# New order lists for the last first-gate steps and the second gate of a Nystrom-attention and two-gate kernel

## The chip, the cores and the metric

One core of a Trainium2 chip runs the whole program. The metric is the device time in microseconds (us) of one execution. The engines are TensorE (PE, with its weight loads PEld), VectorE (DVE), ScalarE (ACT), GpSimd (POOL) and SyncE (SP), which here issues nearly all DMA transfers. A measurement of a change gives the median of several executions.

## The reference, cut to what matters

```python
# attention, Nystrom, per batch (4) and head (8), 576 rows of 64
A, Bm, C = softmax(q @ k_lm.T / 8), softmax(q_lm @ k_lm.T / 8), softmax(q_lm @ k.T / 8)
...
x = (A @ Z @ C @ v)                     # Z: six Newton steps on Bm
x = x.transpose(0, 2, 1, 3).reshape(2304, 512)
h = x @ moe_w_in                        # 512 -> 2048, first gate
x = (h * cos(h)) @ moe_w_out            # 2048 -> 512
h = x @ moe2_w_in                       # second gate
x = (max(h, 0) + alpha * min(h, 0)) @ moe2_w_out
```

Inputs are float32; weights arrive in 64-bit form and are converted on the chip.

## The kernel before, in words

Everything is computed as split float32: each operand is a high part (ACT copy to a rounded float32) and a low part (a subtraction), and each product is three matmuls, high x high, high x low, low x high.

**Order by hand-made list.** The program creates all operations first, each with a key such as `b12:9`: the context before the colon, the running number of the operation within it behind. `Plan.go` (L331) then emits them in the order of the string `ORDER` (L20), one queue for each engine following from it. A suffix `/V`, `/A` or `/G` puts an operation with a choice on DVE, ACT or POOL; without one the first choice of the operation is taken. A tile's buffer is given when its first operation is emitted, in turn within its ring (the lists of `place`, from L428 on), so the order also decides which earlier tile an operation must wait for. Each engine and SP's DMA queue work strictly in list order: a waiting instruction holds back all behind it.

**First gate, contexts t0 to t127 (`tick`, L1087).** A tick makes 128 hidden units for 288 tokens: `t:1` six matmuls into an "h" bank (two banks), `t:2` to `t:7` cos and split on ACT, DVE and POOL, `t:8` to `t:11` three matmuls each into four "acc" banks. Contexts `e` store the sums to the scratch tensor y1d, `c` convert the second gate's weights.

**Second gate, contexts b0 to b39.** The 2304 tokens are cut into four chunks of 512 and one of 256, eight steps each: b0 to b7 chunk 0, b8 to b15 chunk 1 (`btick`, L1744, with `strassen`, L1449), b16 to b31 chunks 2 and 3 (`mtick`, L1546, with `narrow`, L1494), b32 to b39 the last (`mtick`). A step makes 256 hidden units by seven Strassen-like products of six 256-column matmuls each (L1465 or L1509), which must keep their sequence. Copies of partial sums (L409 on ACT, L411 on DVE) and additions on DVE (L1488, L1521) lie between them: in `strassen` the products are numbers 1, 2, 4, 5, 7, 9, 10 and 3, 6, 8, 11 are copies, 12 and 13 additions; in `narrow` the products are 1, 2, 5, 7, 9, 10, 12 and 11 an addition. The activation follows on DVE and ACT, then the second product: for b0 to b15 eight groups of three 512-column matmuls (L1778, numbers 18 to 21 and 26 to 29), later seven products (L1660). In the last chunk a step has two products of twelve matmuls (L1564, numbers 1 and 2) and seven of three (19 to 25).

**Loads of the second gate.** The first chunk makes seven forms of the input weights for every two steps (`s_load`, L1262, contexts s64 to s67): load from wi2d (L1271), high part on ACT (L1251), low part and sums (L414, L1285), and a store of each form to wf2d (L1281). Chunks 1 to 3 load these forms back, 512 KB each (`f_load`, L1307, contexts s68 to s76), into a ring "sr" of seven buffers. So a form's load can start when the last product of the step before has read its buffer. `y_load` (contexts y0 to y4) brings the tokens of a chunk and makes their seven combinations. `load_wo2` (o0 to o15) and `t_make` (x0 to x7, loads at L1413) prepare the output weights; they use a ring "f" of four buffers, which the output copies and stores of chunks 0 and 1 (L1790) use too. In b7, for instance, the four output copies are b7:27, 30, 33, 36 and their stores b7:28, 31, 34, 37.

**End.** `y_end` (L1704) adds the last products on DVE (b39:27 to b39:33, L1720) and stores through SP and ACT.

Of the kernel before, what the change touches and what calls it, by code (L numbers as in the profile page):

```python
# [129 lines left out]
c62:3 t105:7 t108:1 t104:10 t103:9 t106:4 t108:2 t106:5 t106:6 c58:4 t104:9 t103:11 t104:11 t105:11 t108:3 t108:4 t107:1  # L130
t107:2 t107:3 t107:4 t103:8 t105:9 t106:7 t106:11 t108:5 c57:1 t107:5 t107:6 t107:7/V t104:8 t110:1 t105:8 c58:5 t108:6
t110:2 e95:3 c63:2 c62:4 t105:10 t109:1 t110:3 t108:7/V s64:22 c57:2 t110:4 t109:2 t110:5 t110:6 c63:3 t109:3 c57:3
s64:26 t106:9 t106:8 t106:10 t107:11 t108:11 t111:1 t107:8 s64:15 t109:4 t109:5 t111:2 t107:9 t108:9 t108:8 t112:1
t109:6 t109:7/V t109:8 t111:3 t111:4 s64:16 t110:7 t107:10 t108:10 c57:4 t111:5 t109:11 t110:11 t114:1 t112:2 t112:3
t112:4 c63:4 s64:27 t111:6 t112:5 t114:2 t112:6 t113:1 t109:10 t110:10 t109:9 t110:9 t111:7 t111:10 y0:2 t113:2 t113:3
t113:4 s64:28 t112:7 t114:3 t114:4 t110:8 t111:11 t111:8 s64:19 s64:20 t113:5 t114:5 t113:6 e111:5 e111:4 t114:6 t116:1
c57:5 y0:1 t111:9 e111:1/V e111:2/V y0:21 y0:22 t116:2 y0:16 t113:7 y0:3 t115:1 t115:2 t112:11 t112:9 t112:10 s64:17
c63:5 e111:6 y0:4 t114:7 t113:11 t112:8 t113:10 t116:3 t116:4 t116:5 t115:3 t115:4 t115:5 y0:5 s64:13 s64:23 t115:6 y0:7
y0:17 t115:7 t113:8 t117:1 t114:10 t114:11 t119:1 t113:9 t114:9 t114:8 t115:9 t115:8 t115:10 t117:2 t117:3 y0:36 y0:31
t116:6 t119:2 t117:4 y0:23 s64:24/V t119:3 t116:7/V t119:4 y0:11 t117:5 t118:1 y0:12 y0:6/V t119:5 t118:2 t117:6 t117:7  # L140
y0:32/V y0:13/V t118:3 t118:4 t118:5 t118:6 t115:11 t116:11 t116:8 t116:9 t120:1 t117:9 t119:6 t121:1 t118:7 t117:11
t118:11 y0:14 t120:2 t121:2 o1:1 y0:24 s64:21 y0:25 y0:26 y0:33 y0:37/V y0:8/V s64:10 e111:3 t119:7/V t120:3 t116:10
y0:38 t120:4 t120:5 t121:3 t120:6 s65:2 s64:29 t121:4 t121:5 t117:8 t117:10 t121:6 t119:11 o9:1 t122:1 t120:7/V y0:18
t118:9 t119:9 t123:1 o1:2 t122:2 y0:9 y0:29 t121:7/V t122:3 t118:10 t119:10 t118:8 t120:10 t119:8 t122:4 t123:2 y0:10/V
t122:5 t123:3 y0:34 y0:15/V t123:4 t123:5 y0:39 t122:6 y0:35/V o9:2 t122:7 y0:30 y0:19 t123:6 t123:7 t120:8 t120:9
t121:10 t121:9 t124:1 t122:9 t125:1 t121:8 t120:11 t123:9 o1:3 t121:11 t124:2 t124:3 t124:4 t124:5 y0:27 t127:1 t122:8
t125:2 t125:3 t125:4 y0:20 s65:3 o9:3 t125:5 y0:40/V y0:28/V t124:6 t127:2 t127:3 t122:10 t123:10 t122:11 t126:1 t123:8
t124:7/V t124:8 t123:11 t127:4 t127:5 t127:6 t126:2 t125:6 o10:1 c62:5 o11:1 s64:25 s65:1 o0:1 t125:7 t127:7/V t126:3
# [6 lines left out]
b0:25 b0:20 b1:15 b1:22 b1:16 s66:1 b2:11 b0:18 b3:4 b3:5 s66:4 s66:2 b1:23 o6:3 b1:17/G b2:12 b3:3/V s66:11 b1:24 b3:6  # L155
s65:29 e127:6 s66:8 b0:19 b3:7 s66:12/V s66:13 o3:1 e127:3 b2:22 b3:8 s66:5 b3:9 s66:6 b1:25/G s66:9/V s66:14/V s66:15
s66:16/V b2:23 b3:10 b3:11/V b2:14 s66:18/V s66:17 s66:22 s66:10 s65:21 o2:1 b0:26 b1:18 s66:26/V o3:2 s66:27 s66:23
s66:24 b2:15 s66:28/V o12:1 s66:7 b0:28 b3:13 b2:24 b2:16 s66:19 s66:20 s67:2 b0:27 b4:1 b0:29 o2:2 b2:25/G b1:19 b1:21
b4:2 b4:3/V b4:4 b4:5 b1:27 b1:20 b1:28 s67:1 b3:12 b2:17/G s66:29 s66:25 b4:7 b4:6 b1:26 s67:3 b4:8/V b4:9 b4:10 b1:29
b5:1 b5:2 b5:4 s67:4 b4:13 o2:3/V b2:19 b5:5 b3:14 b3:15 o3:3/V s67:8 b3:16 b3:17/G o14:1 s66:21 b4:11/V b5:3/V b2:18  # L160
b2:21 b2:20 b2:27 b2:28 b3:20 s67:5 b3:22 b4:12 b4:22 b3:23 b5:6/V s67:11 s67:12/V b3:24 s67:6 b4:23 s67:9/V s67:14/V
b3:25 b4:14 b5:7 s67:15 b5:8 b5:9 s67:18 s67:22 o13:1 o13:2 s67:16/V o13:3/V s67:26/V b2:29 b3:21 b5:10 b6:1 b3:19 b2:26
b3:18 s67:23 b4:24 o12:2 b6:2 b3:29 b4:15 s67:24/V b5:11 b4:16 o12:3/V o14:2 b5:12 b5:13 o14:3 s67:19 s67:27 b6:4 b3:26
b3:27 b6:3/V b6:5 b6:7 b3:28 s67:20/V s67:28/V b6:6/V b6:8 b6:9 b6:10 b7:1 s67:17 y1:1 b4:25 b4:17 b5:14 b5:15 b5:22
o5:1 o5:2 y1:2 b5:16 y1:3 b6:13 b5:17 b4:20 b7:2 b7:4 b7:5 y1:16 b7:3 b6:11/V b4:21 b4:29 b7:6/V b6:12 b5:23 y1:4 y1:11
y1:5 b6:14 b6:15 y1:17/V s67:25 y1:22 y1:21 s67:21 b7:7 b4:28 b7:9 y1:12/V o5:3 y1:23 y1:24 y1:6 b7:8 y1:36 y1:13/V
y1:25/V y1:31 y1:32/V y1:37/V y1:26/V y1:9 y1:27 o15:1 o7:1 b5:24 b5:25 y1:10/V b7:10 b4:18 b4:19 b7:11 b4:26 b5:21 b8:1
b4:27 b5:19 b5:18 b6:16 b6:17/G b8:2 y1:14 y1:18 y1:19 y1:7 y1:29 o7:2 y1:33/V b6:22 y1:20/V b7:12 y1:38/V y1:15/V y1:39
# [10 lines left out]
b12:5 b9:28 b12:7 b12:6 b12:8 b12:9 b10:20 b12:10 b13:1 b13:2 b13:4 s70:1 b12:11 x6:7 b12:13 x5:3/V x6:6/V x6:9 b12:12
b10:18 b9:27 x6:10/V b12:14 x6:8 y2:2 s70:2 x4:1 x4:2 b10:19 b13:5 x5:4/V b13:3 s70:3 b10:28 x5:5 x5:6 b10:21 b10:29  # L180
b13:7 s70:4 b12:15 b12:16 x5:7 b13:6 b13:9 b12:22 b12:17 b13:8/V b12:23 b10:27 b11:20 b13:10 b10:26 b11:21 b11:18 b11:26
b14:1 b12:24 s70:7 x5:8 x5:9 x5:11 x4:3 x4:4 x4:5 x4:6 x5:12 x4:7 x4:9 b11:19 b14:2 b13:11 b13:12 b13:13 s70:6 x3:2
b14:3/V b13:22 b12:25 x4:10/V b13:23 b14:4 b11:27 x5:10 x4:8 b14:5 y2:1 b14:6 s70:5 b14:7 b13:24 b11:28 b14:9 b14:8
# [1665 lines left out]
```

## Time and profile before

| | |
|---|---|
| runs, median of 3 | 795.76 us (794.31 to 796.95) |
| profiled execution, own time | 791.91 us |
| its span, first to last instruction | 790.1 us |
| granted TensorE clock, mean | 0.999 of full |
| instructions | 18146 |
| DMA | 154.81 MB, mean 196 GB/s |

In the views used below, a line is "line of the source, engine, operation, output tile <- input tile, shape, count". All tiles in SBUF are called m; acc, h and x are PSUM banks. The timeline gives start, duration, and in brackets the engine's idle time before with what ended it. The chain of waits is the run of work that ended last, followed back; "SPq" is SP's issue of a DMA. In the table of stretches each engine has its busy time and, in brackets, its instructions.

### The profile page before, as it was taken

How to read it: one execution, taken by the hardware profiler on the slowest of the kernel's cores; microseconds unless marked ns; L12 is line 12 of the kernel's file. 1: busy time of each engine (PE TensorE's matmuls, PEld its weight loads, DVE VectorE, ACT ScalarE, POOL GpSimd, SP SyncE). 2: the span in 40 equal slices, each digit the busy share in tenths (PEclk: the TensorE clock that was granted, in tenths of full speed). 3: DMA queues.
4: the chain of work that ended last, by engine and by line, in shares of the span. 5: the costliest groups of instructions: out<-in, count | busy, mean ns of one | idle time of the engine just before them, and what ended most of it. 6: DMA issues, size and time to landing. Idle time of an engine off the chain costs nothing. (4 is left out here: it accounts for less than half of the span.)

```text
span 790.1 us, 18146 instructions
## 1 busy us (share of the span) xinstructions
PE 775.1 (98%) x6906; PEld 713.9 (90%) x6906; DVE 637.6 (81%) x1382; ACT 440.3 (56%) x998; POOL 247.5 (31%) x264
## 2 busy tenths in 40 slices
...
GB/s 294 258 277 135 124 162 161 201 200 184 280 196 243 308 167 264 231 213 170 156 213 270 280 205 118 257 244 256 50 214 223 215 47 144 189 204 122 131 199 28
DMA packets 114279, 154.81 MB, mean 196 GB/s; under 512 B 55568, under 2 KB 73488, under 8 KB 114192
## 3 DMA queue, kind: packets, MB, share of 16 engines
...
q10 hardware_dynamic: 160, 0.26, 0.1%
HBM read 114.57 MB, written 39.06 MB: 194 GB/s over the span
## 5 line engine op out<-in xcount | busy, mean ns | idle before, releaser
L414 POOL TENSOR_TENSOR m<-m,m 128x288 fp32r<-128x288 f32 (+4 forms) x183 | 181.8, 1007 | 440.3 <-ACT m L1115 136.0
L1128 PE MATMUL acc<-m,m 128*128 128x288 f32 x1536 | 230.7, 297 | 0.0
L1128 PEld LDWEIGHTS acc<-m,m 128*128 128x128 f32 x1536 | 210.7, 188 | 14.6 <-issue 10.8
L414 DVE TENSOR_TENSOR m<-m,m 128x512 fp32r<-128x512 f32 (+5 forms) x261 | 145.6, 579 | 27.4 <-ACT m L1613 12.3
L1103 PE MATMUL h<-m,m 128*128 128x288 f32 x768 | 124.8, 299 | 0.6 <-DVE m L1113 0.4
L1103 PEld LDWEIGHTS h<-m,m 128*128 128x128 f32 x768 | 108.0, 188 | 7.0 <-DVE m L1113 4.0
L1778 PE MATMUL acc<-m,m 128*128 128x512 f32 x384 | 97.6, 392 | 0.0
L1112 ACT ACTIVATE m<-m,quarter 128x288 f32<-128x288 f32 x128 | 67.5, 534 | 39.7 <-DVE m L1110 39.0
L1509 PE MATMUL x<-m,m 128*128 128x256 f32 x588 | 84.8, 284 | 0.8 <-DVE m L414 0.6
L1778 PEld LDWEIGHTS acc<-m,m 128*128 128x128 f32 x384 | 68.2, 188 | 11.6
L1509 PEld LDWEIGHTS x<-m,m 128*128 128x128 f32 x588 | 75.5, 188 | 3.3 <-ACT m L409 1.0
L1113 DVE TENSOR_TENSOR m<-m,h 128x288 f32<-128x288 f32 x128 | 57.3, 450 | 25.6 <-ACT m L1112 19.9
L1613 ACT ACTIVATE m<-m 128x256 fp32r<-128x256 f32 (+2 forms) x96 | 45.8, 508 | 54.5 <-DVE m L1627 20.5
L1110 DVE SCALAR_TENSOR_TENSOR m<-h,m 128x288 f32<-128x288 f32 x128 | 57.3, 451 | 19.9 <-ACT m L1108 19.0
L1660 PE MATMUL acc<-m,m 128*128 128x256 f32 x485 | 70.0, 283 | 0.1
L1108 ACT ACTIVATE m<-h 128x288 int32<-128x288 f32 x128 | 51.7, 404 | 33.1 <-PE h L1103 31.4
L1115 ACT ACTIVATE m<-m 128x288 fp32r<-128x288 f32 x128 | 55.3, 439 | 26.1 <-DVE m L1113 21.7
L1660 PEld LDWEIGHTS acc<-m,m 128*128 128x128 f32 x485 | 63.2, 191 | 0.5 <-ACT m L1613 0.3
L409 ACT ACTIVATE m<-x 128x256 f32<-128x256 f32 (+6 forms) x80 | 31.1, 399 | 45.4 <-PE x L1509 28.5
L579 DVE SCALAR_TENSOR_TENSOR m<-m,m 128x512 int32<-128x512 int32 x64 | 46.8, 737 | 0.3
L577 DVE SCALAR_TENSOR_TENSOR m<-m,m 128x512 int32<-128x512 int32 x64 | 44.3, 697 | 0.4
L1465 PE MATMUL h<-m,m 128*128 128x256 f32 x300 | 42.7, 281 | 1.2 <-ACT m L409 1.2
(182 smaller groups left out, 1125.6 us busy)
## 6 DMA issues: line engine op xcount, KB each, us to landing
m<-wf2d SPq DMA_DIRECT2D x72, 512.0 KB, 5.0
m<-in_moe_w_in_dram SPq DMA_DIRECT2D x32, 512.0 KB, 6.0
m<-in_moe_w_out_dram SPq DMA_DIRECT2D x32, 512.0 KB, 5.9
wf2d<-m SPq DMA_DIRECT2D x28, 512.0 KB, 4.4
...
```

The source lines that it names most:

```text
L414: ENG[e].tensor_tensor(o, a, b, op=ALU.subtract)
L579: op(dve(512), lambda e: nc.vector.scalar_tensor_tensor(cf.t, rv(0), 29, cf.t, op0=ALU.logical_shift_right, op1=ALU.bitwise_or), r=[raw], ...
L1103: nc.tensor.matmul(out=hp.t[:, 0:CW], lhsT=w_[:, js], rhs=x[:, cs], start=(i == 0), stop=(i == 5))
L1108: op(act(CW, True), lambda e: nc.scalar.activation(k_.t, hp.t[:, 0:CW], AF.Copy, scale=INV2PI, bias=0.25), r=[hp], w=[k_], target=T + 0.8)
L1110: op(dve(CW), lambda e: nc.vector.scalar_tensor_tensor(u.t, hp.t[:, 0:CW], INV2PI, k_.t, op0=ALU.mult, op1=ALU.subtract), r=[hp, k_], w=[u])
L1112: op(act(CW), lambda e: nc.scalar.activation(u.t, u.t, AF.Sin, scale=2.0 * math.pi, bias=quarter), rw=[u], aset="sin")
L1113: op(dve(CW), lambda e: nc.vector.tensor_tensor(hc.t, u.t, hp.t[:, 0:CW], op=ALU.mult), r=[hp, u], w=[hc], target=T + 2.6)
L1115: op(act(CW), lambda e: nc.scalar.activation(gh.t, hc.t, AF.Copy), r=[hc], w=[gh, gl])
L1128: nc.tensor.matmul(out=yg[o].t[:, 0:CW], lhsT=w_.t[:, sl], rhs=x.t, start=(j == ja and i == 0), stop=(j == jb and i == 2),)
L1509: nc.tensor.matmul(out=rv(r), lhsT=a_.t[:, p, c2, js], rhs=b_.t[:, q_, c2], start=(first and c2 == 0 and y == 0), stop=(c2 == 1 and y == 2 ...
L1660: nc.tensor.matmul(out=yb.t[:, 256 * (p + yh):256 * (p + yh) + 256], lhsT=a_, rhs=b_, start=(st and p + yh + y == 0), stop=(en and y == 2) ...
L1778: nc.tensor.matmul(out=ya[n][t].t, lhsT=gv(x_), rhs=r_.t, start=(st and k == 0), stop=(en and k == 2))
```

## The change

Only the string `ORDER` changes, from the 2153rd of its 4254 entries on (in the middle of tick 104). Both lists hold the same operations; 171 of them also change engine: 67 from DVE to POOL, 54 from POOL to DVE, 25 from DVE to ACT and 25 from ACT to DVE. On each engine the operations from the first difference on, before and after, and how many of them can be kept in their relative order: PE 651 and 651 product groups, 328; DVE 677 and 664, 316; ACT 466 and 466, 239; POOL 107 and 120, 41; SP 196 and 196, 93. The diff, cut to whole lines around the steps spoken of below:

```diff
@@ -127,124 +127,124 @@
...
-b0:12 b0:14 o11:3/V o10:3 t125:8 b1:1 o4:1 s65:4 s64:7 t124:10 b1:2 b1:4 b1:5 o0:2 o4:2 s65:8 o0:3/V t126:8 o8:1 b0:15
...
-s65:15 s65:16/V s65:12/V s65:26/V t125:10 t126:10 b1:7 b1:8 b1:9 b1:10 b2:1 t127:8 o8:2 b0:16 o6:2 s65:10 o4:3/V s65:27
-e127:5/V b0:22 s65:28/V s65:17 s66:3 b1:13 t127:9 s65:23 s65:24 s65:19 b1:11/V b1:12 s65:20 t127:10 b2:2 b2:4 b2:3 b2:5
-s65:13 b2:7 b2:6 b2:8 b2:9 b0:17 b2:10 b3:1 b3:2 b0:21 o8:3/V b0:23 e127:2 s65:7 s65:25 b1:14 b2:13 e127:1 e127:4 b0:24
...
-b10:2 s68:7 b7:35 s68:3 b8:23 b7:36/V b10:4 b10:5 s68:6 s68:5 b6:27 b7:26 b7:34 x7:1 b9:15 b10:3/V b10:6 b7:19 b10:7
-b10:8 b7:27 b9:16 b8:24 b10:9 b10:10 b11:1 b11:2 b8:25 b10:11 b11:4 x7:2 b7:37 s69:2 b10:12 b9:17 b9:22 b9:23 b10:13
...
-b10:23 b11:12 x7:8 s69:3 b10:17 b9:21 b9:29 x6:1 x6:2 b8:26 s69:5 b10:24 b10:25 b11:13 x6:3 x6:4 x7:10 b9:18 b9:26
-b11:22 b11:23 s69:6 x6:11 x6:12 b7:31 b11:14 b11:15 x5:1 b11:16 b11:24 b12:1 b12:2 b12:3/V x6:5 x5:2 b11:25 b11:17 b12:4
...
-b17:19 b17:22 b17:23 b17:25 b15:37 x1:2 x1:1 b16:33 b18:7 s71:6 b16:34 b15:27 b18:8 b18:9 b18:10 b16:32 b17:28 b17:26
...
-b27:26 b27:28 b27:21 b28:11 b27:31 b28:12 b28:17 b28:18 b28:13 b26:36 b29:1 b29:2 b26:32 b27:36 b27:27 b27:29 b28:14
...
-b35:25 b37:12 b38:5 b38:6 b38:9 b38:8 b37:15 b37:16 b38:10 b38:13 b38:14 b36:25 b31:51 b39:2 b38:20 b38:11 b38:15 b37:17
...
-b39:13 b39:17 b39:18 b37:25 b37:23 b37:21 b38:19 b37:22 b38:21 b39:19 b38:22 b39:20 b39:14 b39:21 b38:23 b38:24 b39:22
-b39:23 b38:25 b39:24 b39:25 b39:26 b39:27 b39:28 b39:30 b39:29 b39:31 b39:32 b39:34 b39:33 b39:35 b39:37 b39:36
...
+b0:13 b1:1 b1:2 b1:4 s64:7 o4:1 o10:2 o0:2 b1:3 b1:5 b1:7 s65:11 b1:6 s65:8 b0:11/V b0:12 b0:14 b0:15 b0:22 b0:16 t125:9
+t126:9 b0:23 s65:5 t125:10 t124:11 t126:8 s65:9/V s65:12/V b1:8 o4:2 o11:3 o10:3 o0:3 s65:4 s65:6/V s65:14/V s65:18/V
+t126:10 t127:8 b1:9 b1:10 t127:9 o4:3/V o8:1 s65:10 s65:13 o6:1 s65:22/V s65:15 s65:16/V o8:2 s65:26 s65:7 s65:23 b1:11
+s65:19 e127:2/V b1:13 s65:24/V s66:2 b1:12 b0:17 b2:1 b2:2 b2:4 b2:5 e127:1 t127:10 t125:11 t126:11 s66:1 s65:20/V b1:14
+s65:27 s65:28 b2:3 b0:24 o8:3/V b0:25 b2:6 b2:7 b2:9 e127:4/V b1:15 b2:8 o6:2 o6:3/V b1:22 b2:10 b3:1 b3:2 b2:11 b2:13
...
+b8:23 b7:21 b7:35 b7:19 s68:5 b7:29 b7:36/V b8:24 b7:26 b7:27/V b10:4 b9:22 b8:25 b8:21 b10:3 b10:5 b10:6 b10:7 b8:19
+b8:18 b8:26 b10:8 b7:30/V s68:6 b10:9 b10:10 b11:1 b11:2 y2:2 b7:34 b7:37 b7:28 b9:23 b9:14 b9:24 b7:31 b10:13 b10:11/V
+b11:4 b11:5 b11:3 b9:25/G b10:12 b9:15 b9:16 b9:17 b11:7 b10:14 b11:8/V b10:15 x7:2 x7:1 x7:3/V b8:20 x6:2 x6:1 s69:2
+s69:7 s69:1 b10:16 s69:4 b11:6/V b8:28 b8:29 b9:21 b11:9 b9:18 s69:5 b11:10 b8:27 b12:1 b12:2 b9:19 b9:20 b11:13 b10:22
...
+x6:11 x6:4 x6:5 s69:3 x6:6 x6:9 x6:7 x6:8 b12:6 b10:24 b9:27 s69:6 b12:7 b12:8 b12:9 b12:10 x4:2 x4:1 x6:12/V y2:1 b13:1
...
+x0:8/V b17:9 b17:10 b17:11 x0:9 b16:18 b14:27 b15:19 s71:3 b17:12 b16:19 b16:22 b15:20 b16:23 b16:24 b16:28 b16:25
+b15:26 b16:29 x2:8/V b17:13 b16:30 b15:35 b15:32 b18:1 b18:2 b16:26 s71:5 x0:10 b15:29 b17:14 s71:4 s71:6 b16:27 b16:31
...
+b18:7 x1:2 b16:35 b17:19 b17:26 b17:22 b18:8/V b18:9 x1:3/V b18:10 b16:34 b16:33 x1:4/V x1:5 x1:6 b17:21 b17:23 b15:37
...
+b27:27 b23:52 b23:51 b28:12 b27:20 b28:13 b27:29 b26:36 b27:30 b27:31 b27:21 b28:17 y4:8 b28:18 b28:19 y4:1 b29:1 b29:2
...
+b38:3 b38:4 b38:5 b38:7 b37:17 b39:2 b38:8 b38:6 b38:9 b38:10 b38:12 b38:13 b38:11 b39:3 b39:4 b39:7 b38:17 b38:15
...
+b39:8 b39:12 b39:15 b39:16 b38:22 b38:20 b39:19 b39:20 b39:21 b39:17 b39:13 b39:18 b39:26/V b39:14 b38:24 b39:22 b39:23
+b39:27 b39:28 b39:29 b39:31 b39:30 b39:35 b37:25 b38:25 b39:24 b39:32 b39:25 b39:33 b39:37 b39:34 b39:36
...
```

## Rows read from the trace of the kernel before

**Rows 1.** The page, busy time, share of the span and instructions of each engine.
```profile
PE 775.1 (98%) x6906; PEld 713.9 (90%) x6906; DVE 637.6 (81%) x1382; ACT 440.3 (56%) x998; POOL 247.5 (31%) x264
```

**Rows 2.** Busy time by stretch: start:end, length, busy us and (instructions) of each engine, clock, DMA.
```profile
352.00:412.00 60.00, 60.00 (x460) 59.85 (x459) 38.45 (x85) 38.23 (x94) 29.45 (x32) 1.00 0.53 179
412.00:424.00 12.00, 10.28 (x80) 9.66 (x79) 11.70 (x18) 6.78 (x16) 4.29 (x3) 1.00 0.69 250
...
524.00:529.00 5.00, 4.68 (x35) 4.25 (x34) 2.67 (x3) 1.41 (x4) 2.45 (x3) 1.00 0.57 182
...
594.00:598.00 4.00, 3.38 (x28) 3.20 (x27) 3.22 (x7) 2.84 (x6) 2.09 (x3) 1.00 0.60 230
598.00:776.00 178.00, 177.79 (x1472) 176.85 (x1472) 140.70 (x311) 90.47 (x191) 14.31 (x15) 1.00 0.46 158
776.00:786.00 10.00, 9.37 (x72) 8.57 (x71) 7.94 (x25) 2.87 (x8) 0.00 (x0) 1.00 0.00 1
```

**Rows 3.** Page, one group of matmuls; chain of waits, three stretches (start, us, what).
```profile
L1509 PE MATMUL x<-m,m 128*128 128x256 f32 x588 | 84.8, 284 | 0.8 <-DVE m L414 0.6
...
500.87 0.69 PE acc L1778 x3
...
606.69 0.71 PE x L1509 x6
...
775.27 0.36 PE acc L1660 x3
```

**Rows 4.** Timeline, 414 to 422 us: start, us, engine, line, operation [idle before, releaser].
```profile
414.61 0.97 PE L1465 MATMUL h<-m,m 128*128 128x256 f32 x6 [0.20 <-ACT m L409]
...
416.34 0.74 PE L1465 MATMUL h<-m 128*128 128x256 f32 x4 [0.53 <-DVE m L414]
...
418.34 4.29 POOL L414 TENSOR_TENSOR m<-m,m 128x512 fp32r<-128x512 f32 x3 [14.00 <-ACT m L1251]
418.47 1.78 DVE L414 TENSOR_TENSOR m<-m,m 128x512 fp32r<-128x512 f32 x1
...
421.41 0.97 PE L1465 MATMUL h<-m,m 128*128 128x256 f32 x6 [0.99 <-ACT m L409]
```

**Rows 5.** Chain of waits, 517 to 527 us.
```profile
517.46 0.77 POOL m L414
...
518.68 0.37 SPq L1413
...
519.14 0.38 SPq L1307
519.62 7.28 DMA m<-wf2d
```

**Rows 6.** DMA issues (xcount, KB, median us to landing) at 500 and 520 us; tile wf2d, 505 to 530.
```profile
out_dram<-m SPq DMA_DIRECT2D x1, 128.0 KB, 2.3
...
out_dram<-m SPq DMA_DIRECT2D x1, 128.0 KB, 7.2
...
DMA to landing us min/median/max: 3.2/5.6/7.3
```

**Rows 7.** SP's issue at 590.93, PE's wait at 596, and that load's time to landing.
```profile
590.93 0.43 SPq L1307 DMA_DIRECT2D m<-wf2d  x1
...
596.33 0.94 PE L1509 MATMUL x<-m,m 128*128 128x256 f32 x6 [0.62 <-DVE m L414]
...
m<-wf2d SPq DMA_DIRECT2D x1, 512.0 KB, 5.3
```

**Rows 8.** Timeline of PE and of DVE, 667 to 669 us; one of three such places.
```profile
668.28 0.98 PE L1509 MATMUL x<-m,m 128*128 128x256 f32 x6
...
667.54 0.69 DVE L1521 TENSOR_TENSOR m<-x,m 128x512 f32<-128x512 f32 x1
```

**Rows 9.** Chain of waits near the end, from b39:2.
```profile
776.35 1.44 PE x L1564 x12
...
777.82 0.49 DVE m L1588
```

More of the change, by code (lines that the diff above doesn't have):

```diff
@@ L129 @@
 t101:9 t106:1 t104:7/V c56:4 t102:9 t103:10 t102:8 V3:22 t106:2 c60:5 c56:5 c63:1 t105:6 V3:23 t106:3 c58:2 c62:2 c58:3
[L130 to L148, printed above, removed]
@@ L154 @@
-s65:13 b2:7 b2:6 b2:8 b2:9 b0:17 b2:10 b3:1 b3:2 b0:21 o8:3/V b0:23 e127:2 s65:7 s65:25 b1:14 b2:13 e127:1 e127:4 b0:24
[L155 to L168, printed above, removed]
@@ L179 @@
[L179 to L183, printed above, removed]
@@ L184 @@
-b14:10 b15:1 b15:2 b12:20 b15:4 b15:5 b13:14 b12:19 b13:25 x3:1 x3:3/V b14:13 b13:15 x4:11 x4:12 x3:4 x3:5/V b13:16 y2:3
-b14:11 b14:12 b15:3/V b14:14 y2:4/V y2:21 y2:22 b11:29 b12:21 b12:29 y2:16 y2:23 x3:6/V y2:17/V b13:17/G x3:9 y2:36
-b12:18 b15:7 b15:6 b15:8 b15:9 b12:26 b15:10 b13:21 b13:29 y2:24 y2:5 b14:22 x3:10/V b14:15 b14:16 b14:23 b14:24 x3:11
-y2:6/V y2:37/V y2:25/V b12:27 b14:25 b12:28 b13:20 b16:1 x3:7 y2:9 b15:13 x3:8 y2:7 x0:2 y2:11 b15:11 y2:27 x3:12/V
-y2:10/V y2:12/V b15:12 b14:17 y2:26/V y2:13/V b16:2 b13:18 b13:26 b14:21 b15:14 y2:31 y2:32 y2:8/V y2:33/V b16:3 y2:14
@@ L189 @@
-y2:34 y2:28/V x0:1 x0:3 x0:4/V x0:5 y2:15/V y2:35/V y2:29 b16:4 b14:29 b13:28 b16:5 y2:30/V y2:18/V y2:19 b13:19 b16:6
-b16:7 b15:15 b15:16 b16:8 y2:38/V b15:22 b15:23 y2:39 y2:20/V y2:40/V x2:1 b13:27 b16:9 b14:18 x0:6/V b15:17 b14:26
-b16:10 b14:20 b15:18 x2:2 b16:11 b16:12 b16:13 b14:28 b15:24 b15:25/G b16:14 x0:9 x2:3/V x2:4/V x2:5/V b16:15 b17:1
-b17:2 x0:7 b17:3/V b17:4 x2:11 x2:6 b16:17 b16:18 b14:19 b15:21 b17:5 s71:1 b16:16 b17:6 b16:24 b16:19 x0:8 x2:12 b14:27
-b17:7 x2:9 b17:8 b15:26 b17:9 b17:10 b15:20 b15:19 x2:10/V x0:10/V b16:20 b16:21 b16:22 b16:23 b17:11 b16:25 b16:28
@@ L194 @@
-x0:11 x2:7 b16:30 b17:12 b16:29 b17:13 b15:35 s71:3 s71:2 b16:31 x2:8/V b17:14 b18:1 b18:2 b16:26 b15:36/V x0:12/V
-b15:32 b18:3 b16:27 b18:4 b17:15 b17:17 b16:35 b15:29 b18:5 b18:6/V b17:16 b17:24 y3:2 s71:7 s71:5 s71:4 b15:30 b17:18
-b17:19 b17:22 b17:23 b17:25 b15:37 x1:2 x1:1 b16:33 b18:7 s71:6 b16:34 b15:27 b18:8 b18:9 b18:10 b16:32 b17:28 b17:26
-b18:11 b16:36 b18:12 b16:38 b17:20 x1:3 x1:4/V x1:7 x1:8 b17:29 b17:21 b18:13 b17:30 x1:5 b18:17 b15:31 b15:28 b19:1
-b19:2 b17:27 b17:33 b17:31 b17:38 b18:14 b18:15 b18:18 b19:3/V b19:4 b19:5 x1:6/V x1:9 x1:11 b15:33 b19:6/V b17:35 b19:7
@@ L244 @@
-b35:25 b37:12 b38:5 b38:6 b38:9 b38:8 b37:15 b37:16 b38:10 b38:13 b38:14 b36:25 b31:51 b39:2 b38:20 b38:11 b38:15 b37:17
-b39:3 b39:4 b37:18 b37:19 b38:16 b38:12 b39:7 b38:17 b39:11 b39:8 b39:5 b39:6 b39:9 b39:10 b39:12 b39:15 b38:18 b39:16
-b39:13 b39:17 b39:18 b37:25 b37:23 b37:21 b38:19 b37:22 b38:21 b39:19 b38:22 b39:20 b39:14 b39:21 b38:23 b38:24 b39:22
-b39:23 b38:25 b39:24 b39:25 b39:26 b39:27 b39:28 b39:30 b39:29 b39:31 b39:32 b39:34 b39:33 b39:35 b39:37 b39:36
+c62:3 t105:7 t108:1 t104:10 t103:9 t106:4 t108:2 t106:5 t106:6 c58:4 t104:9 t103:11 t105:10 t104:11 t103:8 t107:1 t106:7
@@ new lines @@
+t115:8 t116:8 t117:7/V y0:31 t118:2 y0:11 y0:36 s64:21 t119:6 y0:6/V t118:3 t118:4 t117:9 t117:11 t120:1 t118:5 t120:2
+t120:3 y0:12 t118:6 t119:7 t117:8 y0:32 t118:7 t121:1 t116:10 t117:10 t118:11 t120:4 t120:5 y0:13 t118:10 t119:10 y0:18
+t121:2 c63:5 s65:1 t120:6 s64:29 c62:5 c57:5 s64:10 o1:1 y0:8/V t121:3 t122:1 t118:8 y0:26/V y0:33 t119:11 t121:4 o1:2
+y0:14 y0:37/V t118:9 t121:5 t120:7/V o1:3/V t123:1 t120:11 t121:6 y0:29 t119:8 t120:8 t120:10 t119:9 y0:19 t122:2 y0:27
+y0:28 t122:3 t122:4 t123:2 y0:15/V t122:5 t123:3 y0:20/V t121:7 t123:4 t123:5 t122:6 y0:34 t123:6 t124:1 t120:9 t121:9
@@ new lines @@
+t125:1 t121:11 t121:8 t122:7 t124:2 t122:8 t122:9 t123:7/V t123:9 y0:9 t124:3 t124:4 y0:35 t124:5 t122:11 t123:8 t121:10
+t126:1 t125:2 t124:6 y0:10/V y0:30 t125:3 t125:4 t125:5 t127:1 e111:3 y0:38 y0:39 y0:40 s64:25 o9:1 s65:2 o9:2 t126:2
+t124:7 o9:3 t122:10 t127:2 t126:3 t126:4 t126:5 t125:6 t126:6 o11:1 t123:11 t123:10 t124:10 t124:9 o10:1 t125:7 t127:3
+t126:7 s65:3 b0:1 t124:8 t127:4 t127:5 t127:6 t127:7 o0:1 b0:2 b0:4 o11:2 b0:5 b0:3/V b0:7 b0:6 b0:9 b0:8/V t125:8 b0:10
+b0:13 b1:1 b1:2 b1:4 s64:7 o4:1 o10:2 o0:2 b1:3 b1:5 b1:7 s65:11 b1:6 s65:8 b0:11/V b0:12 b0:14 b0:15 b0:22 b0:16 t125:9
```

143 lines of the change are left out of this document (91 added, 52 removed).

## The prediction

> **What bounds the kernel now.** I read the page's engine line first: TensorE (PE) is busy 98% of the span [rows 1], so an order can only win where PE stands still. The table of busy time by stretch [rows 2] says where that is. Before 352 us the order is unchanged, so I leave that part out. From 352 on, almost every stretch is full; the gaps are 1.72 us in 412 to 424, 0.32 in 524 to 529, 0.62 in 594 to 598, 0.21 in 598 to 776 and 0.63 in 776 to 786. After 786 PE has nothing left: the last stores run out.
>
> These figures are a little low, since a matmul's record outlasts the next one's start. The mean 256-column record is 0.284 us, while six follow each other in 0.71, so 0.12 each [rows 3]. Every gap hides 0.284 - 0.12 = 0.16 us more. With three gaps in 412 to 424, one each at 526 and 595, three in 598 to 776 and two in 776 to 786 (the 0.63 there includes 0.16 after the last matmul): 2.20 + 0.48 + 0.78 + 0.69 + 0.79 = **4.94 us**. That is all the order after 352 us can win, 0.6%. The matmuls and their number stay, and the granted clock is full.
>
> **The change, part by part.** It moves operations and swaps engines for 171 of them; no work is added. From the first changed entry on, TensorE's 651 product groups keep 328 in their old relative order. SP has 196 DMA steps there (93 keep it), POOL goes from 107 to 120 operations, DVE from 677 to 664, ACT keeps 466. I go gap by gap and count product groups between two steps in either list. A group of six matmuls of 256 columns or of three of L1778 takes 0.69 to 0.71 us, three of L1660 take 0.36 [rows 3]; I use 0.70.
>
> *412 to 424.* Three things end late [rows 4]. b1:10 waits for ACT's copy b1:8, with one group between the copy's source (b1:7) and b1:10. b2:1 stops in its middle for DVE: the low half of form A12 (s65:12) sits in DVE's queue behind three sums. b2:7 waits for the copy b2:3, itself behind DVE's b1:13, which stands behind s65:28. The new list puts 8 groups between b1:7 and b1:10 instead of 1, 5 instead of 2 between b2:2 and b2:7, moves s65:12 ahead of the sums, issues the spill store s64:7 before two loads instead of after them, and takes s65:28 off DVE. The postponed first-gate groups (t124 to t127) now fill these waits. Bounds: 0 (three other waits take their place) to 2.20 us; I take 2.0, since every one has three or more groups of new cover.
>
> *526.* b12:9 waits for a load [rows 5]: POOL finishes a subtraction, its "f" buffer comes free, SP issues the two x6 loads queued ahead, then s69:5 and s69:6, and the last lands 7.28 us later. In the new list s69:6 follows form loads only, and has 13 groups from b11:9 to b12:9, two behind the wait on b11:10; 11 x 0.70 = 7.7 us against the slowest landing of this stage, 7.3 [rows 6]. This 0.48 goes.
>
> *But the same hazard moves earlier.* SP now issues stores b7:34, 37, 28, 31, then x7's loads, x6's, and only then s69:2, 7, 1. x6:1 reuses the buffer of b7:31 and must wait until that store has landed; everything behind it in SP's queue waits too. From the end of b7:29 to b12:1 there are 23 groups (16.1 us), to b12:2, which needs s69:1, 24 (16.8 us). The chain: b7:30 on DVE ends 3.5 us after b7:29 (one group of 0.70 for b7:26, then its copy, two steps and b7:30, four of 0.69 at most [rows 8]), 4.9 if two more steps are still ahead; the store lands 2.3 to 7.2 us after issue [rows 6]; two issues of x6 at 0.37 and two form loads ahead of s69:1 at 0.38 make 1.5 [rows 5]; s69:1 lands 3.2 to 7.3 later [rows 6]. Sum 3.5 + 2.3 + 1.5 + 3.2 = 10.5 to 4.9 + 7.2 + 1.5 + 7.3 = 20.9 against 16.8: from 6.3 us of slack to a **stall of 4.1**. The middle, 15.7, passes by one; s69:1 is third of its burst, nearer the late end, so I charge 0.5. What is late next is b14's loads, behind x5.
>
> *595.* b18:12 starts 0.62 us late by its row, at 596.33, while the load s71:6, which stands behind output stores and x1's loads in SP's list, is issued at 590.93 and lands 5.3 us later, just before it [rows 7]. (The row names DVE, L414; that product reads nothing of it, so I hold the DMA for the releaser.) The new list issues s71:6 ahead of the stores and x1; its buffer comes free at b17:10, 19 groups or 13 us earlier. 0.78 us go. Cover gone would cost the same 0.78.
>
> *598 to 776.* Each of the three waits is on a DVE addition of 0.69 with one group (0.71) between its source and its reader; one such reader starts at 668.28 [rows 8]. The new list has three such places too (b25, b27, b28). Nothing goes: 0.
>
> *The end.* b39:20 waits for a chain of steps, first on DVE, that starts where b39:2 ends [rows 9]; the new list brings b39:2 forward, puts 11 groups of 0.36 after it instead of 10, and keeps b37:25 and b38:25 for the end. Bounds 0 to 0.79, I take 0.7. The last addition and store are the same: 0.
>
> *The rest of the reorder.* The first gate's ticks, 352 to 412, show no idle PE now [rows 2]; at least seven of its groups lie between two uses of an "h" bank in both lists, so 0 there, bounds 0 to 1. Form loads for b18 to b28 get at least 6.5 us of TensorE work between buffer release and use, as before, most now 8.6; no gain while they land in time. Against that, groups with one group of cover for a step of another engine are 57 in both lists. As 651 groups stand anew, I charge 0.7 for fresh stalls: as much as the three of [rows 8]; bounds 0 to 2.
>
> *DVE beside POOL.* DVE's s65:28 took 1.78 us while POOL worked on three operations [rows 4]; a 512-wide DVE addition takes 0.69 [rows 8]. With 13 more operations on POOL that can happen more often. The Trainium skill (SBUF — State Buffer, Who interferes with whom) says that a DVE instruction with two SBUF inputs contends with a GpSimd one that reads SBUF; that row agrees. By that rule the sum would come out at -1.4 (rival 3). I put nothing for such contention in the sum, because DVE is busy 81% [rows 1] and can be late without PE waiting, and keep it as a rival.
>
> **Sum:** -2.0 (412) - 0.48 + 0.5 (b12) - 0.78 (595) - 0.7 (end) + 0.7 = **-2.8 us**. Against the profiled execution's 791.91 (span 790.1 and 1.8 around it) that gives 789.1. The runs' median, 795.76, is 3.85 above that execution; where it comes from no row tells. The same step from the median gives **793.0**.
>
> **Rivals.**
> 1. *No change that can be told.* A measurement of this kernel tells about 0.3%, 2.4 us, from no change. If b12 stalls for 1.5 us instead of 0.5, or one wait of 412 to 424 comes back, the sum is about -1.4: 794.4. For it: all that is to be won is 4.94 us. Against: seven of the ten gaps get visible cover.
> 2. *Slower: SP's queue at b12 and b14.* The chain above at its late end costs 4.1 at b12; x6's conversions then end late, x5's loads wait for their buffers, and s70's form loads stand behind x5 in the same way, as much again. 8.2 - 0.5 - 2.8 = +4.9: 800.7. It decides against the change once the two stalls pass 0.5 + 2.8 + 2.4 = 5.7 us together, so store b7:31 must land about as late as the latest here. For it: stores of this stage took 7.2 us. Against: in the new list the four stores go out with few loads around them, as the one that took 2.3.
> 3. *DVE and POOL in each other's way.* 13 x (1.78 - 0.69) = 14 us more on DVE, from [rows 4, 8]; if a tenth reaches TensorE's waits, +1.4: 794.4.
> 4. *Better than summed.* Loads here landed just in time (b12, b18). If the typical run's 3.85 us are late transfers, the new list saves some of them: 791.
>
> **Chances.** My forecast with rival 4: 0.48 faster by over 0.3%. Rivals 1 and 3, and the forecast falling just short: 0.36. Slower: 0.16, rival 2 nearly alone. Range: low 790.0, all 4.94 us and 0.8 of rival 4; high 797.5, a little over half of the way to rival 2. It leaves out the worse half of rival 2 and a little below.
>
> **What would show it.** Right: PE's idle from 412 to 424 under 0.5 us, none at b18:12, under 0.4 in the last 12 us, and three short waits on L1521 between 600 and 776. Wrong: in the stretch of b12 (about 515 to 530) or b14, PE waiting for the DMA of wf2d by over 1 us, SP issuing s69:2 only after a store's landing; or new waits on L414 where DVE and POOL overlap.

## The result: slower by 0.6%

The new order takes 798.78 us (median of 14 runs, 796.57 to 801.26), the order before 793.98 (14 runs, 791.23 to 797.35): ratio **1.0059, interval 1.0045 to 1.0073**, about 4.7 us slower where 2.8 us faster was forecast. Here and below, a ratio and its 95% interval come from all runs of a kernel against runs of the kernel before that were taken alongside it; the latter's median is 793.85 us for e1 to e4, 794.43 for e5 and e6 and 792.90 for e7 to e9, so two medians of different rows can't be set side by side.

The profiled execution of the new order (801.26 us, span 799.2) is the slowest of the 14. Its page, the line that answers to [rows 1]:

```profile
PE 778.0 (97%) x6906; PEld 715.0 (89%) x6906; DVE 638.1 (80%) x1369; ACT 440.2 (55%) x998; POOL 262.2 (33%) x277
```

PE does the same 6906 matmuls, and its share of the span falls from 98% to 97%. A row of the unchanged part, in the timeline of PE, ahead of the first moved entry, and the last three matmuls:

```profile
347.83 1.09 PE L1059 MATMUL x<-m,m 64*32 64x512 f32 x16
...
793.86 0.52 PE L1660 MATMUL acc<-m,m 128*128 128x256 f32 x3
```

The same two groups start at these times in the trace of before:

```profile
343.99 1.09 PE L1059 MATMUL x<-m,m 64*32 64x512 f32 x16
...
785.33 0.52 PE L1660 MATMUL acc<-m,m 128*128 128x256 f32 x3
```

So 3.84 us of the two profiles' difference lie ahead of the change, in code that is the same; that varies from run to run and is not the change's. The changed part grows by 793.86 - 347.83 - (785.33 - 343.99) = **4.69 us**, close to the measured difference of the runs. From here on I compare this *changed part*, counted from t104:1 (0.62 us ahead of that L1059 group) to the start of the last matmul (0.23 us behind the start of its group of three): 442.19 us before, 446.89 after.

Where the 4.7 us are, in the table of busy time by stretch (start:end, length, then busy us and instructions of PE, PEld, DVE, ACT and POOL, clock, DMA share, GB/s):

```profile
352.00:424.00 72.00, 71.99 (x555) 71.64 (x553) 53.12 (x107) 46.88 (x113) 32.35 (x35) 1.00 0.53 182
424.00:524.00 100.00, 100.00 (x630) 90.30 (x629) 77.37 (x123) 37.42 (x81) 44.63 (x40) 1.00 0.69 241
524.00:598.00 74.00, 73.92 (x470) 65.98 (x469) 60.14 (x106) 34.50 (x80) 38.18 (x39) 1.00 0.50 169
598.00:740.00 142.00, 141.65 (x1169) 140.58 (x1168) 109.83 (x224) 78.60 (x163) 6.24 (x7) 1.00 0.49 168
740.00:770.00 30.00, 25.90 (x204) 25.50 (x203) 22.42 (x62) 7.58 (x19) 2.59 (x2) 0.94 0.46 141
770.00:795.00 25.00, 23.25 (x183) 22.01 (x182) 18.99 (x57) 6.47 (x18) 0.00 (x0) 1.00 0.07 22
```

The gaps of [rows 2] in 412 to 424, 524 to 529 and 594 to 598 are gone: 0.09 us are left between 352 and 598. But from 740 to 770, the last chunk, PE stands for 4.10 us where it stood at most 0.21 in all of 598 to 776 before, and there its granted clock is 0.94. PE's waits from 350 us on (releaser: us in total, times, longest) name them:

```profile
PE x L1564 <- DVE m L1588: 2.3, 1, 2.3
PE x L1564 <- DVE m L1591: 1.7, 1, 1.7
PE acc L1660 <- DVE m L414: 1.1, 2, 0.6
```

In the kernel before, this view has no wait on L1588 or L1591. In the timeline of PE these two waits are b33:2 and b35:2, with the rows around them:

```profile
745.60 1.59 PE L1564 MATMUL x<-m,m 128*128 128x256 f32 x12
748.94 0.98 PE L1564 MATMUL x<-m 128*128 128x256 f32 x6 [1.75 <-DVE m L1591]
...
759.38 2.93 PE L1564 MATMUL x<-m,m 128*128 128x256 f32 x12 [2.35 <-DVE m L1588]
762.11 0.74 PE L1660 MATMUL h<-m,m 128*128 128x256 f32 x3
762.69 0.51 PE L1660 MATMUL acc<-m,m 128*128 128x256 f32 x3
```

And in the timeline of DVE the steps that released them:

```profile
747.61 0.42 DVE L414 TENSOR_TENSOR m<-m,m 128x256 fp32r<-128x256 f32 x1
747.94 0.48 DVE L1588 TENSOR_SCALAR m<-x,alpha_sb 128x256 f32<-128x256 f32 x1
748.46 0.42 DVE L1591 SCALAR_TENSOR_TENSOR m<-x,m 128x256 f32<-128x256 f32 x1
...
758.52 0.42 DVE L1682 TENSOR_TENSOR m<-acc,m 128x256 f32<-128x256 f32 x1
758.85 0.48 DVE L1588 TENSOR_SCALAR m<-x,alpha_sb 128x256 f32<-128x256 f32 x1
```

A step of the last chunk puts its two products side by side into one "x" bank: `b:1` into columns 0 to 255, `b:2` into 256 to 511 (L1564). `b:3` and `b:4` (L1588, L1591) read the first half, `b:5` and `b:6` the second. `b:2` uses no result of `b:3`. In the order before, each of b32 to b39 lists `b:2` ahead of `b:3`; the new one lists b33 as 1, 3, 4, 2 and b35 as 1, 3, 2. Both products then start just behind the end of the reads listed ahead of them (748.88 and 759.33), and those reads run only when DVE's in-order queue comes to them, behind sums of the chunk before (L1682) and low parts (L414).

The second wait has a tail. The clock table of PE (length, PE busy and matmuls, clock, DMA share, GB/s):

```profile
757.00:759.00 2.00, 0.04 (x1) 1.00 0.84 250
759.00:760.00 1.00, 0.62 (x3) 0.59 0.42 148
760.00:762.00 2.00, 2.00 (x11) 0.50 0.00 0
762.00:764.00 2.00, 2.00 (x17) 0.85 0.34 80
```

PE comes back at the lower clock level (0.50, 1.2 GHz): its twelve L1564 matmuls take 2.93 us instead of the 1.59 of 745.60, the next three 0.74 instead of 0.51: another 1.6 us.

My theory (A): the two waits and the half clock, 1.9 + 2.5 + 1.6 = 6.0 us, are the loss, they come from the order of `b:2` and `b:3` in the list alone, and the head of the change gains what was forecast. Rival B: the head loses in the typical run, by SP's queue at b12 and b14 (rival 2 of the prediction), and the profile happened to miss it. Rival C: DVE is late in the last chunk anyway, whatever the list says. Rival D comes up with e5.

### The profile page after: what moved, and what is told of

The parts are those of the page before. It is cut to its first block, busy times and chain, and to the rows that moved or that the text cites. A ratio compares the mean times of both kernels' runs of the same rounds, so it can differ in the third digit from the quotient of the medians.

```text
span 799.2 us, 18167 instructions
## 1 busy us (share of the span) xinstructions
PE 778.0 (97%) x6906; PEld 715.0 (89%) x6906; DVE 638.1 (80%) x1369; ACT 440.2 (55%) x998; POOL 262.2 (33%) x277
## 4 chain that ended last, share of the span: by engine, by line
PE 74%; DVE 12%; DMA 5%; ACT 5%; issue 2%; SPq 2%; POOL 0%; DVEq 0%; ACTq 0%
PE acc L1128 20%; PE acc L1778 10%; PE h L1103 10%; PE x L1509 9%; PE h L1465 6%; PE acc L1660 6%; PE x L1465 4%; PE h L1660 3%; PE x L1564 2%; DVE m L414 2%; PE x L1059 2%; DMA m<-in_moe_w_in_dram 1%; PE x L1660 1%; SPq L656 1%; DVE m L1113 1%
## 5 line engine op out<-in xcount | busy, mean ns | idle before, releaser
L414 POOL TENSOR_TENSOR m<-m,m 128x288 fp32r<-128x288 f32 (+4 forms) x193 | 193.4, 1015 | 433.5 <-ACT m L1115 144.8
L414 DVE TENSOR_TENSOR m<-m,m 128x512 fp32r<-128x512 f32 (+4 forms) x251 | 143.9, 595 | 20.3 <-ACT m L1613 9.8
L1778 PE MATMUL acc<-m,m 128*128 128x512 f32 x384 | 95.6, 392 | 0.0
L1613 ACT ACTIVATE m<-m 128x512 fp32r<-128x512 f32 (+2 forms) x96 | 46.2, 510 | 58.9 <-DVE m L1627 27.5
L1110 DVE SCALAR_TENSOR_TENSOR m<-h,m 128x288 f32<-128x288 f32 x128 | 57.3, 451 | 17.5 <-ACT m L1108 16.8
```

Source lines behind the costliest of these rows:

```text
L414: ENG[e].tensor_tensor(o, a, b, op=ALU.subtract)
L1110: op(dve(CW), lambda e: nc.vector.scalar_tensor_tensor(u.t, hp.t[:, 0:CW], INV2PI, k_.t, op0=ALU.mult, op1=ALU.subtract), r=[hp, k_], w=[u])
L1778: nc.tensor.matmul(out=ya[n][t].t, lhsT=gv(x_), rhs=r_.t, start=(st and k == 0), stop=(en and k == 2))
```

## The experiments

**e1: the two products back ahead of the reads.** The rest of the order stays as changed.

```diff
-b32:17 s79:2 b32:16 b33:3 s79:3 b33:4 b33:7 b33:8 b33:2 b33:5
+b32:17 s79:2 b32:16 b33:2 b33:3 s79:3 b33:4 b33:7 b33:8 b33:5
...
-b35:3 b33:18 s81:1 b32:22 b32:24 b35:2 b33:24
+b35:2 b35:3 b33:18 s81:1 b32:22 b32:24 b33:24
```

> The changed order with two entries moved: b33:2 ahead of b33:3 and b35:2 ahead of b35:3, so that the second product of an x bank is again listed before the reads of its first half. Theory A (the two waits of L1564 on L1588/L1591 are the loss): both vanish, 1.9 + 2.8 us, and the 1.2 us go in which TensorE ran at half clock behind the second, so 798.8 - 5.9 = 792.9, about 1.0 below the kernel before. Rival B (the loss is in the head, SP's queue of b12 and b14 in the typical run): no change, 798 to 799. Rival C (DVE is late there anyway): the waits turn up under another name, less than 1.5 us come back, 797.3 or more.

Measured: 794.12, ratio 0.9997 (0.9978 to 1.0017); the changed part 441.22 us, 5.67 below the new order. PE's waits from 350 us on:

```profile
PE acc L1660 <- DVE m L414: 1.1, 2, 0.6
```

Both waits on L1588 and L1591 are gone and none has taken their place. Two moved list entries give back all of the loss. In the list b33:2 passes only DVE and SP entries, so its move changes no engine's queue, and its wait goes all the same; b35:2 passes two groups of three matmuls in PE's queue (b32:22 and b32:24). C falls.

**e2: b35:2 alone.** b33:2 stays behind its reads.

> The changed order with b35:2 alone moved ahead of b35:3; b33:2 stays behind b33:3 and b33:4. Theory A: the 2.8 us wait goes and the half clock behind it (1.2 us), the 1.9 us of b33:2 stay: 794.8; the granted clock is 1.00 throughout 750 to 780. If the half clock comes from something else, only 2.8 go: 796.0. Rival B: 798 to 799.

Measured: 797.14, ratio 1.0043 (1.0024 to 1.0062); changed part 444.55. That is 2.34 below the new order where 4.0 were expected. The wait at b35:2 is gone, but now the half clock stands behind b33:2, whose wait is the same 1.74 us as in the new order, where the clock stayed full:

```profile
746.63 1.43 PE L1564 MATMUL x<-m 128*128 128x256 f32 x6 [1.74 <-DVE m L1591]
747.86 1.48 PE L1564 MATMUL x<-m,m 128*128 128x256 f32 x6
```

```profile
746.00:748.00 2.00, 1.37 (x7) 0.73 0.92 180
748.00:750.00 2.00, 2.00 (x12) 0.50 0.44 178
750.00:752.00 2.00, 2.00 (x17) 0.92 0.66 203
```

So the wait was sized rightly, but the half clock does not belong to the wait at b35:2 alone: 446.89 - 444.55 is about that wait of 2.5, with one half clock gone and another come.

**e3 and e4: head and tail apart.** One list as far as b23:2 (about 640 us), then all entries not yet listed in the order of the other.

> The changed order up to b23:2 (about 640 us), behind it the order of the kernel before. Theory A: the head's gains alone, 3.5 us of gaps filled and 0.4 of fresh ones, so 3.0 below the kernel before: 791.0. Rival B: the head holds the loss, 797 or more.

> The order of the kernel before up to b23:2, behind it the changed order. Theory A: the loss alone, without the head's 3.0 us: 798.8 + 3.0 = 801.8. Rival B: about the kernel before, 793 to 795.

e4: 801.29, ratio 1.0099 (1.0064 to 1.0134), as theory A has it. Its view of PE's waits holds the old head's gaps and the new tail's together:

```profile
PE x L1564 <- DVE m L1588: 2.3, 1, 2.3
PE x L1564 <- DVE m L1591: 1.7, 1, 1.7
PE h L1465 <- ACT m L409: 1.2, 2, 1.0
PE acc L1660 <- DVE m L414: 1.1, 2, 0.6
PE x L1509 <- DMA m<-wf2d: 0.6, 1, 0.6
PE h L1465 <- DVE m L414: 0.5, 1, 0.5
```

Here the clock stays at 1.00 behind both waits, so its changed part (447.79) is only 0.9 above the new order's.

e3: 794.18, ratio 1.0010 (0.9991 to 1.0028); changed part 441.55. Not the 797 of B, but not the 791 of A either. Its waits show why:

```profile
PE x L1509 <- DVE m L1521: 1.6, 2, 1.1
PE h L1660 <- DVE m L414: 0.4, 1, 0.4
```

The first row is the joint: two waits on DVE behind the cut, at 640.87 and 653.12, 1.9 us with their records' overlap; neither stands in the traces of before, of the new order or of e6. (At the joint one product, b21:38, reads a form buffer that b22:30 has written anew, so a part of the third chunk is computed from another form.) The joint was badly chosen, so e3 does not tell A's size; e6 repeats it.

**e5: the last ticks.** e1 leaves waits of 0.76 us (at b36:21) and 0.70 (at b39:19) on low parts and a short one of 0.21 at b39:20, more than the 0.57 (at b37:25) and 0.22 (at b39:20) of the order before; the overlap of records is counted in. Three entries move:

```diff
-b36:19 b36:21 b31:51 s82:3 b37:13 b36:25 b35:23 b38:1 b35:22 b38:2 b36:23 b37:10 b37:7 b37:8 b37:14
+b36:19 b31:51 s82:3 b37:13 b36:25 b35:23 b38:1 b36:21 b35:22 b38:2 b36:23 b37:10 b37:7 b39:2 b37:8 b37:14
...
-b37:17 b39:2 b38:8 b38:6 b38:9 b38:10 b38:12 b38:13 b38:11 b39:3 b39:4 b39:7 b38:17 b38:15 b37:18
+b37:17 b38:8 b38:6 b38:9 b38:10 b38:12 b38:13 b38:11 b39:3 b39:4 b38:17 b38:15 b39:7 b37:18
```

> The order with both products ahead of the reads (b33:2, b35:2), and three entries more moved: b39:2 ahead of b37:8 (it stood 14 entries later), b36:21 six entries later behind b38:1, b39:7 two entries later behind b38:15. Theory A: the last waits of 0.76, 0.70 and 0.21 us on the low parts (L414) get more work in front of them and go; from the change's first entry to the last matmul 441.2 - 1.7 = 439.5 us against 442.2 of the kernel before, ratio 0.997. Rival D (those waits only move on to the next product in the last ticks): 441.2, ratio 0.9997 again.

Measured: changed part 439.31, and the view of PE's waits from 350 us on is empty (the short ones on L1521 are below what it lists). D falls. The whole run, 793.22, ratio 0.9986 (0.9970 to 1.0002), gains less than that; in the profiled run the unchanged part alone was 5.45 us longer than in that of before, 3.26 of it in one place:

```profile
198.78 2.44 PE L1059 MATMUL x<-m,m 64*32 64x512 f32 x16 [3.26 <-ACT m L817]
```

That wait is absent in the traces of before and of e6 and stands in e1's with 2.8 us: a run-to-run matter ahead of the change, which stays open here. It is why I read each step from the changed part, and the ratio only with its interval.

**e6: e3 with the joint at b31:12, about 728 us.** The list is the new one as far as b31:12; all entries not yet listed follow in the old order.

> The changed order up to b31:12 (about 728 us), behind it the order of the kernel before, so that all of the last chunk is the old one and the joint lies in a place where the two lists hold nearly the same. Theory A: the head's gains without the tail's loss: 3.46 us of gaps filled, 0.41 of fresh ones and 0.3 more in the short waits on L1521, so 442.2 - 2.75 = 439.4 from the change's first entry to the last matmul, ratio 0.9965. Rival B (the head holds the loss): above 1.003.

Measured: 791.63, **ratio 0.9962 (0.9947 to 0.9976)**; changed part 440.19, 2.00 below before where 2.75 were expected. B falls, and the head's gain is shown. This order is the new one up to the last chunk, and it beats both kernels, the one before by 0.4%. One row of waits is left, the old end's:

```profile
PE h L1660 <- DVE m L414: 0.4, 1, 0.4
```

**e7: e6 with b39:2 fourteen entries earlier.**

```diff
-b34:25 b36:23 b35:25 b37:12 b38:5 b38:6 b38:9 b38:8 b37:15 b37:16 b38:10 b38:13 b38:14 b36:25 b31:51 b39:2 b38:20
+b34:25 b39:2 b36:23 b35:25 b37:12 b38:5 b38:6 b38:9 b38:8 b37:15 b37:16 b38:10 b38:13 b38:14 b36:25 b31:51 b38:20
```

> The order of e6 (the changed one up to b31:12, behind it that of the kernel before) with b39:2 fourteen entries earlier, ahead of b36:23. The waits of 0.58 and 0.23 us in front of b39:20 go as they went with the new tail: 440.2 - 0.8 = 439.4 us from the change's first entry to the last matmul, against 442.2 before; ratio 0.996. If b39:20's chain is bound elsewhere: 440.2 and 0.997.

Measured: changed part 438.85, 3.34 below before, and PE's waits are empty in the view as in e5. The whole run: 791.84, ratio 0.9979 (0.9957 to 1.0001). By the changed part it is the best order, by whole runs not to be told from e6. Why it helps stands in the trace of before. In the chain of waits b39:1 ends at 772.75; in the timeline b39:3, which reads only what b39:1 wrote, starts at 777.82, right behind the end of b39:2 (776.35 + 1.44, [rows 9]), and DVE stands idle for it with the low parts queued behind:

```profile
771.33 1.43 PE x L1564 x12
```

```profile
777.82 0.48 DVE L1588 TENSOR_SCALAR m<-x,alpha_sb 128x256 f32<-128x256 f32 x1 [1.50 <-PE x L1564]
778.34 0.42 DVE L1591 SCALAR_TENSOR_TENSOR m<-x,m 128x256 f32<-128x256 f32 x1
778.68 0.75 DVE L414 TENSOR_TENSOR m<-m,m 128x256 fp32r<-128x256 f32 x2
779.15 0.39 PE L1660 MATMUL h<-m,m 128*128 128x256 f32 x1 [0.41 <-DVE m L414]
```

So the order of accesses to a bank binds the other way too: a read listed behind a write of the other half waits for the write. The old end's wait came through it, and in e7 DVE's idle time before b39:3 is 0.43 instead of 1.50.

**e8: the hazard kept, the reads sooner.**

```diff
-b31:49 b31:50 b31:46 b32:12 b33:1 b32:17 s79:2 b32:16 b33:3 s79:3 b33:4 b33:7 b33:8 b33:2
+b32:12 b33:1 b32:17 s79:2 b33:3 s79:3 b33:4 b33:7 b33:8 b33:2 b31:49 b31:50 b31:46 b32:16
```

> The changed order with b31:49, b31:50, b31:46 and b32:16, DVE steps that stand in front of b33:3 or b33:4, moved behind b33:4; b33:2 stays behind the reads in the list. Theory A (the product waits for the reads, and the reads for DVE's queue): the reads run as soon as b33:1 ends, 0.48 and 0.42 us with their latencies, so the wait at b33:2 falls from 1.75 to about 1.1; the one at b35:2 stays 2.35. If the wait were on the bank's earlier use or a load, it would stay at 1.75.

A single run, 797.12:

```profile
746.68 0.98 PE L1564 MATMUL x<-m 128*128 128x256 f32 x6 [1.03 <-DVE m L1591]
```

The wait falls from 1.75 to 1.03, that at b35:2 stays at 2.35. Both reads now follow b33:1 at once, so the 1.03 is the two reads themselves. So the list's order makes the wait, and DVE's queue makes its length. The changed part is 2.2 us below the new order's, 0.7 of it by the wait; the rest is about the half clock, which is absent here.

**e9: the price of rival 2.** e7 with one load later in SP's queue.

```diff
-s69:2 s69:7 s69:1 b10:16 s69:4 b11:6/V b8:28 b8:29 b9:21 b11:9 b9:18 s69:5
+s69:2 s69:7 b10:16 s69:4 b11:6/V b8:28 b8:29 b9:21 b11:9 b9:18 s69:5 s69:1
```

> The order of e7 with the load s69:1 issued two places later in SP's queue, behind s69:4 and s69:5. Rival 2's price: in six traces s69:1 lands within 0.1 to 0.7 us of the start of b12:2; two issues later it should land some 2 us later, and TensorE waits 1.4 to 2.0 us there. If the landing is not what b12:2 starts on, no wait.

A single run, 791.94; b12:2 in the timeline of PE:

```profile
519.39 0.88 PE L1465 MATMUL h<-m 128*128 128x256 f32 x6
521.70 0.98 PE L1465 MATMUL h<-m,m 128*128 128x256 f32 x6 [1.43 <-DMA m<-wf2d]
```

By the trace's issue times the load went out 1.5 us later against b12:1 than in e7, and PE waited 1.43. Not all of that is the later issue: in e7 the load landed 1.46 us ahead of b12:2, and in e9 it also took 7.2 us to land instead of 5.7. The chain of rival 2 is real: b12:2 starts when this load lands. The new order runs along its edge without falling over it; the load lands 0.14 us ahead of b12:2 in its trace, 0.04 in e2's and up to 1.5 in the others with this head.

The changed part of all kernels, worked out as above, and the whole runs:

| kernel | changed part, us | ratio of whole runs, 95% interval |
|---|---|---|
| before | 442.19 | 1 |
| after | 446.89 | 1.0059 (1.0045 to 1.0073) |
| e1 both products first | 441.22 | 0.9997 (0.9978 to 1.0017) |
| e2 b35 only | 444.55 | 1.0043 (1.0024 to 1.0062) |
| e3 new head, old tail | 441.55 | 1.0010 (0.9991 to 1.0028) |
| e4 old head, new tail | 447.79 | 1.0099 (1.0064 to 1.0134) |
| e5 e1, last ticks | 439.31 | 0.9986 (0.9970 to 1.0002) |
| e6 new head, old last chunk | 440.19 | 0.9962 (0.9947 to 0.9976) |
| e7 e6, b39:2 earlier | 438.85 | 0.9979 (0.9957 to 1.0001) |
| e8 reads sooner | 444.67 | one run |
| e9 late load | 440.11 | one run |

## Why the prediction was wrong

**The step that failed** is "The rest of the reorder", where I charged "0.7 for fresh stalls", bounds 0 to 2. I had counted, for every product, how many groups stand between it and the steps that make its operands or free its buffer. I never compared the order of a bank's reads and writes. `b:2` and `b:3` share no operand and no half of the bank, and the kernel's own bookkeeping keeps the halves as two buffers (`w=[Xq[x]], hold=[X]`), so no count of groups could see an edge between them. The program as it runs has one: a product listed behind a read of its bank waits for that read, whichever half it reads (e1 and e8 show it). Measured, this is 6.0 us in the profiled run, three times my upper bound, and 4.4 without the half clock, as in e4. One row that I had read showed the edge: in [rows 9] b39:3 (L1588 at 777.82) starts where b39:2 ends though it reads only b39:1's half (e7), and b33:3 and b37:3 of that trace start 0.04 us behind the end of b33:2 and b37:2 in the same way. I took the chain as it stood and did not ask why it began there. The Trainium skill (PSUM — Partial Sum Buffer, PSUM bank collisions raise a hardware error) says that TensorE's write and VectorE's read of one bank must not meet on the same partitions even at different columns, and that PSUM is to be guarded by bank and 32-partition quadrant, simply by bank, not by address. The waits at 748.94 and 759.38 agree; whether the chip would err without them was not tried.

The gains, one by one:

- *412 to 424*, forecast -2.0: all three waits went, -2.2.
- *526*, forecast -0.48: gone.
- *b12 through SP's queue*, forecast +0.5: 0. The reckoning held closely, though: "the middle, 15.7, passes by one" of 16.8. In the new order's trace x6:1 was issued 0.1 us after store b7:31 had landed, as that chain had it, and s69:1 landed 0.1 us before b12:2 started; e9 shows what a late landing costs there. The middle of that range said 0, and the 0.5 that I charged towards its late end was not due.
- *595*, forecast -0.78: gone. s71:6 lands 8 us ahead of its use instead of just in time. In e4, which keeps the old head, the view puts this wait down to the DMA of wf2d, as I had held.
- *598 to 776*, forecast 0, and *fresh short stalls*, +0.7: the three short waits of 0.23 became five of 0.23 to 0.30 and one of 0.17, together 1.4 against 0.7: +0.7, as charged.
- *The end*, forecast -0.7: wrong in sign. I counted 11 groups behind b39:2 instead of 10, but the low parts of b36 and b39 came later in DVE's queue: 1.65 us against 0.79, +0.9. e7, which moves b39:2 alone, shows that it was the right entry for the old end's waits and had to come 14 places earlier; in the new end it was moved together with two others (e5), so its share there is not shown.
- *DVE beside POOL* (rival 3): DVE has 13 instructions fewer and is as busy as before; the table of busy time over the changed part, first before, then after:

```profile
343.00:786.00 443.00, 439.50 (x3242) 418.32 (x3241) 345.84 (x697) 215.77 (x481) 112.52 (x112) 1.00 0.52 178
```

```profile
347.00:795.00 448.00, 441.71 (x3241) 420.00 (x3241) 346.20 (x684) 215.21 (x481) 126.93 (x125) 1.00 0.52 176
```

By the records of the instructions, the 586 steps that run on DVE in both orders behind the first changed entry took 325.1 us instead of 319.0, 6.1 more where I had priced 14. It goes with POOL: 68 of them ran beside a POOL operation only in the new order and took 12.7 us longer, 62 only in the old one and took 9.1 less, and the 385 that did so in neither differ by 0.1 in all. It hardly reaches PE: e5 and e7, with the same or nearly the same assignment in the head, show no wait of PE on DVE beyond the short ones above and one of about 0.3 in e5 (b4:9, on L411).

Sum of what was forecast, with its measured sizes: -2.2 - 0.5 - 0.8 + 0.7 + 0.9 = -1.9; with the 6.0 it is +4.1 of the measured 4.7. The last 0.6 is spread over small steps that I did not follow. Where the list is kept as forecast, the size holds: without the end's 0.7 my sum is -2.1, and e6, which keeps the old end, shows -2.0; with it -2.8, and e7, with its end mended, shows -3.3. That -2.1 meets -2.0 is in part luck: by its measured terms e6 should stand at -2.2 - 0.5 - 0.8 + 0.7 = -2.8, and my undue 0.5 for b12 happens to stand in for most of what is missing. The base is a smaller matter: 795.76 was the median of 3 runs, over 14 it is 793.98.

**The rivals.** Rival 2 put the slower side into SP's queue; the slower side came from a mechanism that none of them named, and what I named as signs of a wrong prediction were L414 and wf2d, not L1588 or L1591. The high end, 797.5, left it out. The 0.16 for slower was the price of the one queue I had looked at.
